# A convolution by blocked Fourier transforms: the second copy of the weights loaded in four transfers of 49 partial rows

## Chip, cores and metric

The kernel runs on one core of one Trainium2 chip. The metric is the device time of one execution in microseconds (us). Lower is better.

## What is computed

The input `x` has the shape 1 x 224 x 224 x 96, the weights `w` the shape 7 x 7 x 96 x 96, both bf16. The reference pads the weights to the image size, transforms both, multiplies per frequency with a sum over the input channels, and transforms back:

```python
wp = jnp.pad(w, ((0, H - K), (0, W - K), (0, 0), (0, 0)))
Xf = rfft2(x, axes=(1, 2)); Wf = rfft2(wp, axes=(0, 1))
Yf = jnp.einsum('bhwi,hwio->bhwo', Xf, Wf)
y = irfft2(Yf, s=(H, W), axes=(1, 2)).astype(bfloat16)
```

This is a circular 7 x 7 convolution with 96 input and 96 output channels.

## The kernel before

The kernel transforms only along the image rows' axis (height), in eight blocks of 28 output rows each, and does the width axis as short sums over the seven taps. The width of 224 is cut into seven strips of 32 columns (`t` = 0 to 6). For each strip TensorE first multiplies the rows of `x` with a table `Fm` (tiles `x0` and `xh`, which live in the last slots of `WF` and are shown as `WF` in the profile, and `xn`), and ScalarE or VectorE copy the result to `xf`. VectorE forms sums and differences of `xf` in the `J` tiles. In 17 rounds per strip (`b_round`, one for each frequency) TensorE multiplies `xf` and `J` with the transformed weights `WF`. The result `yf` goes to a scratch tensor in DRAM (`scr`), comes back with another arrangement (`tt`), is multiplied with the table `Gm`, and is stored to `out`.

The transformed weights are made at the start. The 49 taps of `w` are 49 rows of 96 x 96 elements, 18,432 bytes each. They are loaded twice into the tile `wq` (`wqx` in the code), which has 128 partitions:

- The first copy stands in partitions 30 to 78 (from `W1`). Twelve wide jobs (`wide_jobs`, line 397) read partitions 0 to 78 of it with a table of factors and fill the weights of the first frequencies.
- The second copy stands in partitions 79 to 127 (from `K1`). It is shifted by 48 columns, so that its row has 9,168 elements (`WC`, 18,336 bytes) instead of 9,216. The jobs of `prep_jobs` (line 415) read all 128 partitions and so both copies at once, eight output channels in four matmuls. They make the weights of the later frequencies.

Both copies are loaded by two helpers. `load_w` (line 192) moves `n` whole rows in one transfer. `load_last` (line 196) moves the last row, cut into 16 runs, in two transfers of half a run each. The kernel before calls each with 48 rows and the last row.

All these loads are issued by SyncE (SP) on its one queue, in the order of the code: first half of the rows of strip 0 (`x0`), the first copy, the halos, the other half of strip 0, the two halves of strip 1 (`xn`), and as the last the second copy. Each half of a strip is a transfer of 112 rows and one of 6 rows. After the second copy the queue holds the first stores of `yf`.

TensorE's order is written out in the code (the `_Ordered` wrapper keeps each engine's program order). Warm-up matmuls, the transforms of strip 0 and the wide jobs come first. Then the rounds start, and other jobs are placed between them by `pace` (line 786): a list of jobs is given a first and a last step, and the jobs are spread evenly over the steps between. The first of the `prep_jobs` comes at step 4, in the third round, with the transforms of strip 1 around it. Its matmul is TensorE's first reader of the second copy.

The profile puts nearly all instructions on line 101, the line of the wrapper, so groups are told apart by their tiles.

Of the kernel before, what the change touches and what calls it, by code (L numbers as in the profile page):

```python
# [66 lines left out]
def kernel(  # L67
# [7 lines left out]
    _, H, W, C = x.shape  # L75
# [5 lines left out]
    PW = KT * KT  # L81
    FR = 2 * NS
    EP = 128
    K1 = W1 + PW
    assert K1 + PW == EP and len(S5) == PGRP[0][1]
    C2 = C // 2
# [59 lines left out]
    def dma(out_ap, in_ap):  # L146
        return DE.dma_start(out=out_ap, in_=in_ap)
# [18 lines left out]
    wqx = wtmp.tile([128, C - 1 + 127 * C + 1], BF16, name="wq")  # L166
    WC = C * C - C2
# [19 lines left out]
    def load_x(t, jg):  # L187
        return load_rows(xbuf(t, jg), jg, t * 2 * TW, 2 * TW)

    wsrc = w.rearrange("kh kw i o -> (kh kw) (i o)")  # L190

    def load_w(p, k, n, h):
        m = (C * C, WC)[h]
        return dma(wqx[p:p + n, 0:m], bass.AP(wsrc.tensor, wsrc.offset + k * C * C + h * C2, [[C * C, n], [1, m]]))

    def load_last(p, h):
        n = (C * C, WC)[h]
        m = n // 16
        for a, b in ((0, m // 2), (m // 2, m)):
            dma(wqx[p:p + 1, 0:n].rearrange("p (c m) -> p c m", c=16)[:, :, a:b],  # L200
                bass.AP(wsrc.tensor, wsrc.offset + (PW - 1) * C * C + h * C2 + a, [[C * C, 1], [m, 16], [1, b - a]]))

    load_x(0, 0)
    load_last(K1 - 1, 0)
    load_w(W1, 0, PW - 1, 0)
    for jg in range(2):
        load_rows(xh_bufs[jg], jg, W - PAD, PAD)
    load_x(0, 1)
    for jg in range(2):
        load_x(1, jg)  # L210
    load_w(K1, 0, PW - 1, 1)
    load_last(EP - 1, 1)

    wu = cpool.tile([128, 128], BF16, name="wu")
    wur = wu[:].unsqueeze(1).to_broadcast([128, 4, 128])
# [717 lines left out]
    for i, (g, q) in enumerate(order):  # L933
# [3 lines left out]
        k = i + 8 - LF  # L937
# [37 lines left out]
```

## Time and profile before

| What | Value |
|---|---|
| median of 3 runs | 270.6 us (270.03 to 270.99) |
| profiled execution, its own time | 269.31 us |
| its span from first to last instruction | 267.5 us |
| granted TensorE clock, mean | 0.995 |
| PE (matmul) busy | 255.1 us, 95% |
| DVE busy | 216.2 us, 81% |
| ACT busy | 197.6 us, 74% |
| first copy, issue of its whole rows | 864.0 KB in one transfer |
| second copy, issue of its whole rows | 859.5 KB in one transfer |
| issue of the second copy's three transfers on SP | from 11.69 us, 3.29 us in all |

Times in the profile count from the start of the span. PE is TensorE's matmul, PEld its weight load, DVE VectorE, ACT ScalarE, POOL GpSimd, SP SyncE. In a timeline, the bracket behind a piece is the time that the engine stood idle before it, and what ended that; "issue" is a wait that the profile can't name. A table of windows gives for each stretch its length, the busy time and count of each engine, the granted clock, and at the end the mean busy share of the 16 DMA engines and the GB/s. A packet's bytes and its time are counted where it starts, so a share can pass 1 in a short window.

### The profile page before, as it was taken

The page shows a single profiled execution, that of the slowest core. Times are in us where ns is not written, and L with a number is a line of the kernel's source. Part 1 is how long each engine was busy: PE and PEld are TensorE (multiplying, and loading weights), DVE is VectorE, ACT ScalarE, POOL GpSimd, SP SyncE. Part 2 cuts the span into 40 slices and gives each one's busy share as a digit, 9 for nine tenths or more (in the row PEclk, how much of TensorE's full clock was granted, in tenths as well). Part 3 has the DMA queues.
Part 4 walks back from the last instruction along what each step waited for, and adds up shares of the span by engine and source line. Part 5 has one row for each costly group of instructions (what it writes and reads, how often), then busy time and mean ns, then how long its engine had stood idle before and what let it go on. Part 6 is the DMA issues. An engine that isn't in the chain of part 4 may idle for free. (4 is left out here: it accounts for less than half of the span.)

```text
span 267.5 us, 12139 instructions
## 1 busy us (share of the span) xinstructions
PE 255.1 (95%) x5128; PEld 235.7 (88%) x5128; DVE 216.2 (81%) x465; ACT 197.6 (74%) x485; POOL 97.7 (37%) x152
## 2 busy tenths in 40 slices
PE   8897999999999999999999999999999999999983
PEld 2787999999998999999999998989999889879861
DVE  7997699889899788778887888778888789978523
ACT  8796978497964578998988789886988864187123
POOL 7771324364558344222222322233123323422100
PEclk9999999999999999999999999999999999999998
DMA  8994102711111697987876486979678443887845
GB/s 197 230 251 76 48 2 67 245 45 48 47 48 49 192 258 159 294 238 223 272 195 188 117 235 221 253 216 341 235 152 242 169 128 125 204 250 182 259 107 191
DMA packets 46690, 46.78 MB, mean 175 GB/s; under 512 B 35292, under 2 KB 38056, under 8 KB 46540
## 3 DMA queue, kind: packets, MB, share of 16 engines
q1 hardware_dynamic: 44348, 43.95, 59.6%
q10 hardware_dynamic: 2288, 2.06, 2.6%
q8 instruction: 40, 0.66, 1.1%
q14 instruction: 14, 0.11, 0.2%
HBM read 24.66 MB, written 21.33 MB: 172 GB/s over the span
## 5 line engine op out<-in xcount | busy, mean ns | idle before, releaser
L101 PE MATMUL pb<-WF,J 96*128 96x96 bf16 x2821 | 162.9, 206 | 1.7 <-DVE J L101 1.3
L101 PEld LDWEIGHTS <-J 96*128 96x128 bf16 x2821 | 138.0, 98 | 12.3 <-issue 3.5
L101 POOL TENSOR_TENSOR yf<-v,u 128x384 bf16<-128x384 f32 x79 | 81.3, 1040 | 145.7 <-issue 84.6
L101 ACT CAST xf<-pb 96x408 bf16<-96x408 f32 (+3 forms) x145 | 67.3, 486 | 7.6 <-PE pb L101 3.8
L101 PE MATMUL pb<-WF,xf 96*128 96x96 bf16 x952 | 60.0, 206 | 0.9 <-ACT WF L101 0.9
L101 DVE TENSOR_TENSOR J<-xf 96x1824 bf16<-96x1824 bf16 (+1 forms) x84 | 56.9, 716 | 0.0
L101 PEld LDWEIGHTS <-xf 96*128 96x128 bf16 x952 | 47.2, 98 | 1.3 <-issue 1.2
L101 PE MATMUL pb<-Fm,xn 118*128 118x136 bf16 (+3 forms) x640 | 45.5, 199 | 0.2 <-DVE u L101 0.2
L101 PE MATMUL pb<-tt,Gm 102*84 102x384 bf16 (+1 forms) x132 | 32.9, 326 | 0.6 <-ACT J L101 0.3
L101 PEld LDWEIGHTS <-xn 118*128 118x128 bf16 x640 | 30.3, 97 | 0.3 <-issue 0.3
L101 ACT CAST WF<-pb 96x480 bf16<-96x480 f32 (+1 forms) x58 | 28.6, 558 | 2.3 <-PE pb L101 2.3
L101 ACT CAST J<-pb 84x384 bf16<-84x384 f32 (+1 forms) x65 | 28.1, 490 | 2.6 <-PE pb L101 2.6
L101 ACT CAST yo<-pb 84x384 bf16<-84x384 f32 (+1 forms) x63 | 27.1, 486 | 2.3 <-POOL yf L101 1.3
L101 DVE TENSOR_TENSOR J<-J 96x912 bf16<-96x912 bf16 (+2 forms) x42 | 24.2, 576 | 0.0
L101 PE MATMUL pb<-wq 128*128 128x120 bf16 (+1 forms) x288 | 21.8, 226 | 0.7 <-DMA wq<-in_w_dram 0.6
L101 PEld LDWEIGHTS <-wq 128*128 128x128 bf16 (+1 forms) x288 | 19.9, 148 | 1.7 <-DVE xf L101 1.1
L101 DVE TENSOR_TENSOR yf<-v,u 128x384 bf16<-128x384 f32 x26 | 15.1, 580 | 0.9
L101 PE MATMUL pb<-wu 128*112 128x384 bf16 (+1 forms) x59 | 14.5, 391 | 1.1 <-DVE ct L101 1.1
L101 PEld LDWEIGHTS <-wu 128*112 128x112 bf16 (+1 forms) x59 | 7.4, 127 | 5.6 <-issue 3.1
L101 PEld LDWEIGHTS <-Gm 102*84 102x84 bf16 (+1 forms) x132 | 11.1, 117 | 1.0 <-issue 0.4
L101 ACT COPY xf<-xf 96x816 bf16<-96x816 bf16 (+3 forms) x20 | 11.1, 613 | 0.0
L101 ACT CAST tt<-pb 112x384 bf16<-112x384 f32 x8 | 3.6, 480 | 9.3 <-PE pb L101 9.2
(387 smaller groups left out, 239.2 us busy)
## 6 DMA issues: line engine op xcount, KB each, us to landing
scr<-yf SPq DMA_DIRECT2D x30, 288.0 KB
xn<-in_x_dram SPq DMA_DIRECT2D x12, 672.0 KB
tt<-scr SPq DMA_DIRECT2D x24, 336.0 KB
out_dram<-yo SPq DMA_DIRECT2D x12, 252.0 KB
out_dram<-J SPq DMA_DIRECT2D x12, 252.0 KB
tt<-scr SPq DMA_DIRECT2D x6, 288.0 KB
WF<-in_x_dram SPq DMA_DIRECT2D x2, 672.0 KB
out_dram<-tt SPq DMA_DIRECT2D x8, 168.0 KB
```

Of the source, the lines that this page charges most:

```text
L101: r = fn(*a, **k)
```

## The change

The second copy is loaded by four transfers. Each moves all 49 rows (partitions 79 to 127) and a quarter of the columns, 2,292 elements or 4,584 bytes per row. The two transfers of the last row's pieces go away for this copy. `load_w` gets the column bounds as arguments. The first copy is loaded as before.

```diff
-    def load_w(p, k, n, h):
-        m = (C * C, WC)[h]
-        return dma(wqx[p:p + n, 0:m], bass.AP(wsrc.tensor, wsrc.offset + k * C * C + h * C2, [[C * C, n], [1, m]]))
+    def load_w(p, k, n, h, m0=0, m1=C * C):
+        return dma(wqx[p:p + n, m0:m1], bass.AP(wsrc.tensor, wsrc.offset + k * C * C + h * C2 + m0, [[C * C, n], [1, m1 - m0]]))
...
-    load_w(K1, 0, PW - 1, 1)
-    load_last(EP - 1, 1)
+    for i in range(4):
+        load_w(K1, 0, PW, 1, i * WC // 4, (i + 1) * WC // 4)
```

## Prediction

> **What bounds the kernel now.** I read the page first, then the windows by stage, the waits of PE, and the timeline around the first reader of the second copy. The page's first lines name the bound:
>
> ```profile
> span 267.5 us, 12139 instructions
> PE 255.1 (95%) x5128; PEld 235.7 (88%) x5128; DVE 216.2 (81%) x465; ACT 197.6 (74%) x485; POOL 97.7 (37%) x152
> ```
>
> From 27.3 to 233 us PE waits for named things this often and no more (the waits of PE in that window), and it is busy for 203.70 of the 205.80 us (windows by stage: length, PE, PEld, DVE, ACT, POOL, clock, DMA share, GB/s):
>
> ```profile
> PE pb L101 <- DVE J L101: 1.3, 3, 0.5
> PE pb L101 <- DVE u L101: 0.4, 2, 0.2
> 27.20:233.00 205.80, 203.70 (x4345) 194.32 (x4346) 174.11 (x362) 160.35 (x404) 75.91 (x76) 1.00 0.60 170
> ```
>
> So what PE gains or loses near 27 us reaches the end nearly one for one: the chain that ended last runs over PE until 239.10 us, then over the last stores and loads of the scratch. The place that the change touches is in the timeline:
>
> ```profile
> 23.67 0.41 PE L101 MATMUL pb<-Fm,WF 118*128 118x40 bf16 x10
> 25.30 0.50 PE L101 MATMUL pb<-Fm,WF 118*128 118x32 bf16 x14 [1.23 <-issue]
> 26.59 0.35 PEld L101 LDWEIGHTS <-J 96*128 96x128 bf16 x7
> 27.20 0.81 PEld L101 LDWEIGHTS <-wq 128*128 128x128 bf16 x12 [0.25 <-DMA wq<-in_w_dram]
> ```
>
> The reader is to see two things. The first reader of the second copy really waits for its load: PE is ready at 26.95, the last completion is at 27.14 in the trace's landing records, the load starts at 27.20. The copy is 0.25 us late today, so any lateness is paid by PE. And 1.9 us earlier PE stands 1.23 us on "issue".
>
> **On how many engines a transfer runs.** In the first 31 us the DMA view counts
>
> ```profile
> DMA packets 1102, 5.06 MB, mean 163 GB/s; under 512 B 228, under 2 KB 528, under 8 KB 1000
> ```
>
> No data packet there is under 512 B, so 228 are completion writes, one per engine used: six transfers of 112 rows and two of 48 with 16 each, six of 6 rows with 6, four of 16 pieces with 16, 96 + 32 + 36 + 64 = 228. For other row counts I take the page's 35,292 packets under 512 B: 32,384 are 384-byte pieces (scratch reloads: 24 x 112 x 8 + 6 x 68 x 12 + 12 x 34 x 4 + 2 x 72 x 16 + 32 x 16 + 2 x 96 x 8) and 200 are 56-byte pieces of GA and GB. That leaves 2,708, which is exactly what comes out if every transfer uses the largest divisor of its rows up to 16 (84 rows 14, 34 rows 2); one engine per row up to 16 would give 3,000. So **49 rows run on 7 engines**, and 48 ran on 16. [...]
>
> **The change part by part.**
> *Removed:* one transfer of 48 x 18,336 B (3 rows per engine) and two of 16 pieces. *Added:* 4 x 49 packets of 4,584 B, 28 per engine on seven engines: 898,464 B / 7 = 128.4 KB instead of 55 KB each. Order and number of instructions on PE, DVE, ACT and POOL stay; the first reader waits on four semaphores instead of three, which I cost at nothing (below 0.05 us).
>
> *SP:* three issues took 3.29 us from 11.69 with a wait in them; a fourth is 0.3 to 0.6 us (issue rows) and ends near 15.5. That is hidden, for the DMA engines come to the second copy only from 17.2 (first 18,336 B packet). Behind it SP has a store that it can't issue before 31.29. If that cover were gone, 0.6 us.
>
> *When the seven engines can start.* The packet records show nine engines with their first packet of the second copy from 17.24 to 17.86 and seven from 19.16 to 20.85. [...] From 18.0 each late engine has about 4.3 rows of 6 KB left; today they go at 12 to 16 GB/s beside nine engines that already write the second copy. [...]
>
> *Rate of one engine.* Nothing before shows seven engines on this data alone. Bounds from windows, GB/s / (16 x share):
>
> ```profile
> 4.20:9.60 5.40, 5.05 (x106) 3.40 (x104) 4.74 (x17) 4.86 (x7) 4.25 (x22) 1.00 0.98 211
> 9.60:17.20 7.60, 7.00 (x115) 6.26 (x114) 7.02 (x14) 5.76 (x13) 5.99 (x26) 1.00 1.04 263
> 20.90:26.00 5.10, 3.87 (x115) 3.79 (x113) 3.25 (x7) 3.03 (x10) 0.78 (x1) 1.00 0.34 55
> 22.70:26.00 3.30, 2.07 (x66) 1.99 (x64) 2.03 (x4) 2.03 (x7) 0.00 (x0) 1.00 0.25 50
> 144.50:146.00 1.50, 1.50 (x38) 1.50 (x36) 1.47 (x3) 1.31 (x5) 0.00 (x0) 1.00 0.28 103
> ```
>
> First copy 13.5; rows of `x` with all engines busy 15.8; second copy today 10.1, its last part, on the late engines, 12.5; a tail with some 4.5 engines busy 23.0. I take 23.0, since only seven of 16 engines will be busy: the last second-copy packet that ran nearly alone took 0.749 us (24.5 GB/s), so the data itself is not slow. [...]
>
> [...]
>
> *Sum.* From the last packet to completion takes 1.2 us today (25.93 to 27.14). 19.4 + 128.4 / 23.0 (5.6) + 1.2 = **26.2 us**, 0.9 us before today's landing. PE gains the 0.25 us wait. What is late next is "issue": PE's fetch queue (q8, 40 packets of 16 KB, 256 instructions each) had a packet from 22.28 that took 1.69 us, where undisturbed ones take 0.95; PE stood until 25.30. If that packet's engine is not among the seven, up to 0.74 us of the stall goes too. Bounds 0 and 0.74; I take 0.15, because VectorE is behind PE there (busy 28.87 of 32.80 us from 27.20 to 60.00) and would hand part of it back, and because a landing at 26.2 leaves nothing to spare. Total -0.25 - 0.15 = -0.4 us, so 268.9 for the profiled execution (269.31: span 267.5 and 1.8 around it). It lies 1.3 below the median; set on the median, **270.2 us**.
>
> **Rivals.**
> 1. *The seven engines become the bound (slower).* Lateness is nothing until the landing passes 27.14, that is below 128.4 / 6.54 = 19.6 GB/s. At 15.8 the landing is 28.7 (+1.6 us, 272.2); at 13.5, 30.1 (+3.0, 273.6); at 12.5, 30.9 (+3.7, 274.3); at 10.1, 33.3 (+6.2, 276.8). For it: these are the rows of this stage, the last-but-one with this very data and about seven engines. Against: the 0.749 us packet, and the nearly empty queues. [...]
> 2. *The fetch stall goes as well (faster).* -0.25 - 0.74 = -1.0, 269.6. For it: the fetch lengthened just when the second copy's large packets were under way. Against: the landing must then come by 26.2.
> 3. *The transfers use 16 engines after all.* Then the load is as today: 0 to -0.25, 270.5. Against: the count of 2,708.
>
> **How the numbers follow.** 0.3% is 0.8 us, about what a measurement of this kernel can tell from no change. Forecast (landing before about 28, part of the fetch stall) 0.40, rival 3 0.03, both within 0.3%. Rival 1 by more than 0.8 us (below 17.5 GB/s): 0.34. Rival 2, more than 0.8 us gained: 0.23. Range: down to 269.4, rival 2 and a little; up to 273.5, rival 1 at 13.5 GB/s, which leaves the slower rows outside with about 0.12 and 0.08 below. The likeliest case's own range is 269.8 to 271.4.
>
> **What would show it.** Right: 208 packets under 512 B in the first 31 us (228 - 48 + 28; 16 engines would give 244); the first weight load from `wq` with 128 partitions without a DMA wait before it; no DMA traffic but fetches after some 25.5 us. The fetch step: "issue" before the 25.30 matmul falls from 1.23 to about 0.5. Wrong: a wait on "DMA wq<-in_w_dram" of over 1 us in front of that load, with DMA traffic at 70 to 110 GB/s until 28 us or later.

## Result and the profile after

| | Before | After |
|---|---|---|
| first pair: median of 6 and 6 runs | 270.47 us (269.08 to 272.44) | 268.0 us (266.91 to 268.23) |
| ratio | | 0.9896, 95% interval 0.9854 to 0.9937 |
| profiled execution: time, span, granted clock | 269.31, 267.5, 0.995 | 267.92, 266.1, 0.999 |

The change made the kernel faster. The changed kernel was run in two more sets, beside new runs of the kernel before: 0.9954 [0.9921, 0.9987] and 0.9934 [0.9902, 0.9967]. The first ratio is the most favourable of the three. The granted clock differs a little between runs, on average 0.9953 in 90 runs of the kernel before and 0.9972 in 29 of the changed one; executions in the chip's slower state are left out of these averages, the ratios and the fits. A fit to the spans of 192 runs of this study, with one term for each kernel and one for the granted clock, gives the change -1.03 us (standard error 0.16) at equal clock, about -0.4%; the same fit to the device times gives -1.20 (0.17).

The clock term may take away part of the effect: in the two first profiles the granted clock is 1.00 until TensorE has done its last matmul (262.79 and 261.34 us) and falls to 0.50 only after it, at 264.88 and 265.34, so the mean also depends on how long the kernel goes on from there. Without the clock term the fits give -1.39 (0.22) on the spans and -1.56 (0.22) on the device times. The gain is thus some 1.0 to 1.6 us. Single differences of one microsecond between two profiles mean little here; stages have to be compared.

The page of the changed kernel, its first lines:

```profile
span 266.1 us, 12141 instructions
PE 254.9 (96%) x5128; PEld 235.7 (89%) x5128; DVE 216.2 (81%) x465; ACT 197.3 (74%) x485; POOL 98.3 (37%) x152
```

The DMA view of its first 31 us:

```profile
DMA packets 1198, 5.06 MB, mean 163 GB/s; under 512 B 208, under 2 KB 476, under 8 KB 1144
q1 hardware_dynamic: 1192, 4.97, 60.0%
```

The 208 small packets are the prediction's 228 - 48 + 28: by this count, one small packet per engine and transfer, each of the four transfers runs on seven engines. The packets of the data queue q1 took 60.0% of the time of 16 engines in the window; before it was 70.7%, for the same bytes.

The timeline at the place of the change (start, duration, engine, work, and in the bracket the idle time before it):

```profile
23.20 0.76 PE L101 MATMUL pb<-Fm,WF 118*128 118x40 bf16 x24
23.80 0.63 PE L101 MATMUL pb<-Fm,xn 118*128 118x64 bf16 x16
...
24.78 0.46 PE L101 MATMUL pb<-WF,J 96*128 96x96 bf16 x7
26.32 0.81 PEld L101 LDWEIGHTS <-wq 128*128 128x128 bf16 x12 [1.22 <-issue]
26.35 0.92 PE L101 MATMUL pb<-wq 128*128 128x120 bf16 x12 [1.11 <-DMA wq<-in_w_dram]
```

The stall of 1.23 us on "issue" ahead of the 25.30 matmul is gone: no piece from 23.20 to 24.78 has a bracket. PE now arrives at the first reader of the second copy 1.11 us early and stands there until the copy lands. The idle time has changed its place and its cause, and the reader starts at 26.35 instead of 27.23. The windows by stage (length, PE, PEld, DVE, ACT, POOL, clock, DMA share, GB/s) show the copy on seven engines in the second and third row. The kernel before moved 55 and 50 GB/s there, the changed one moves 113 and 87 with about the same busy share of the engines (0.32 and 0.26 against 0.34 and 0.25), so each busy engine moves 2.2 and 1.7 times as much (an estimate from these shares):

```profile
9.60:17.20 7.60, 7.13 (x121) 6.64 (x120) 7.42 (x15) 6.09 (x13) 5.99 (x26) 1.00 1.02 265
20.90:26.00 5.10, 4.34 (x127) 4.19 (x124) 3.26 (x7) 4.49 (x12) 0.42 (x1) 1.00 0.32 113
22.70:26.00 3.30, 2.54 (x76) 2.39 (x72) 2.50 (x5) 3.16 (x9) 0.00 (x0) 1.00 0.26 87
27.20:233.00 205.80, 203.72 (x4349) 194.16 (x4347) 174.68 (x363) 159.39 (x402) 75.91 (x76) 1.00 0.60 171
```

The waits of PE from 27.2 to 233 us are the same as before:

```profile
PE pb L101 <- DVE J L101: 1.3, 3, 0.5
PE pb L101 <- DVE u L101: 0.4, 2, 0.2
```

Because PE executes the same 5,128 matmuls in the same order in every kernel here, the start of the n-th matmul cuts all executions into the same stages. The table gives the stages of one profiled execution each, in us (matmul 120 lies in the work on the first copy, 400 just behind the first reader of the second, 5050 at 250 us):

| Kernel | start of 120 | 120 to 800 | 800 to 5050 | 5050 to last |
|---|---|---|---|---|
| before | 11.16 | 32.74 | 205.70 | 12.86 |
| before, second profile | 11.01 | 32.33 | 205.74 | 12.67 |
| changed | 10.73 | 32.31 | 205.71 | 12.26 |
| changed, second profile | 10.54 | 32.84 | 205.73 | 13.16 |
| changed, third profile | 11.19 | 31.26 | 205.73 | 13.04 |
| 49 whole rows, one transfer | 10.88 | 31.65 | 205.75 | 13.57 |
| changed, copy issued earlier | 10.77 | 31.34 | 205.72 | 12.74 |
| the same, second profile | 11.02 | 31.37 | 205.70 | 13.40 |

Two things follow. Between 800 and 5050 the rows shown agree within 0.05 us, so what PE wins near 27 us it keeps to 249 us. Of the other runs, only the one with 48 rows in quarters differs by more than a tenth: its profile has 206.58 us there, with a wait of 0.7 us for `tt` from the scratch that no other profile has. And the first and last stage vary by 0.7 and 1.3 us between executions of kernels that do the same there: of the 1.4 us between the two first spans, 0.43 is there before the change can act, 0.43 belongs to the stage of the change and 0.60 to the tail, where the wait for `xf` from the scratch was 0.3 instead of 0.9 us.

### The profile page after: what moved, and what is told of

It reads as the page before. It is cut to its first block, busy times and chain, and to the rows that moved or that the text cites. A ratio compares the mean times of both kernels' runs of the same rounds, so it can differ in the third digit from the quotient of the medians.

```text
span 266.1 us, 12141 instructions
## 1 busy us (share of the span) xinstructions
PE 254.9 (96%) x5128; PEld 235.7 (89%) x5128; DVE 216.2 (81%) x465; ACT 197.3 (74%) x485; POOL 98.3 (37%) x152
```

## Experiments

**The kernel before, unchanged.**

> The kernel before, unchanged, timed against itself and profiled again. It shows how the two places that changed (the stall on issue ahead of the 25.30 us matmul, 1.23 us, and the wait for the second copy, 0.25 us) vary from one execution to the next, and the spans of its timed runs. Theory E (engines): the seven late engines include the one that fetches PE's instructions, so a stall of 0.8 to 1.5 us plus a wait of 0 to 1.5 us is in every execution; the first reader of the second copy starts between 27 and 29 us. Theory N (mostly noise): the first reader moves by over 1 us between executions for reasons at the start of the kernel, and the ratio 0.9896 is half noise. Ratio expected 1.000 by both.

Measured: 270.15 us, ratio 1.002 [0.9977, 1.0063], so the comparison shows no difference where there is none. Its first reader starts at 26.45, ahead of the 27 to 29 us of theory E, since the copy landed in time in this execution. Its timeline has the stall again, with another size:

```profile
24.83 0.50 PE L101 MATMUL pb<-Fm,WF 118*128 118x32 bf16 x14 [0.91 <-issue]
```

**The changed kernel, unchanged.**

> The changed kernel, unchanged, timed again on the same chip as the others. Theory E: ratio 0.988 to 0.994, first reader near 26.3 us with no stall on issue before it. Theory N: ratio 0.995 to 0.998, first reader anywhere from 26 to 27.5 us.

Measured: 268.57 us, ratio 0.9954 [0.9921, 0.9987]. No "issue" stall; the wait for `wq` was 1.50 us and the reader started at 26.71. The place is as theory E expected it, but the ratio lies in the range of theory N: the first ratio was probably in part noise.

**One transfer of 49 whole rows**: the count of engines without the packet size.

```diff
-    for i in range(4):
-        load_w(K1, 0, PW, 1, i * WC // 4, (i + 1) * WC // 4)
+    load_w(K1, 0, PW, 1, 0, WC)
```

> One part of the change alone: 49 whole rows in one transfer, so seven engines, but packets of 18,336 B instead of quarters. Theory E (what counts is which engines carry the copy): as the changed kernel, ratio 0.988 to 0.994, no stall on issue near 24 us, landing near 26.3 us. Theory P (what counts is the size of the packets that the instruction fetch has to queue behind): the stall stays at 0.8 us or more and the ratio is 0.995 to 1.000.

Measured: 268.29 us, ratio 0.9932 [0.99, 0.9965]; at equal clock -1.17 us (0.25). The small packets are 208 - 28 + 7 = 187, one transfer on seven engines. No "issue" stall, and a wait of 0.40 us at the reader:

```profile
25.82 0.97 PE L101 MATMUL pb<-wq 128*128 128x120 bf16 x12 [0.40 <-DMA wq<-in_w_dram]
```

The column quarters are not needed for the gain. The row count is enough.

**48 rows in four column quarters**, the last row in pieces: the packet size without the count of engines.

```diff
-    load_w(K1, 0, PW - 1, 1)
+    for i in range(4):
+        load_w(K1, 0, PW - 1, 1, i * WC // 4, (i + 1) * WC // 4)
```

> The other part alone: 48 rows in four column quarters on 16 engines, with the last row in pieces as before; packets of 4,584 B. Theory E: the copy is as slow as before (nine engines early, seven late, landing 26.5 to 28 us), the stall on issue stays near 1.2 us, ratio 0.998 to 1.003. Theory P: the fetch packet near 22 us is as short as with the change (1.1 us instead of 1.7), the stall falls below 0.5 us, ratio 0.990 to 0.996.

Measured: 269.21 us, ratio 0.9969 [0.9937, 1.0001], between the two theories; at equal clock -0.26 us (0.24). The DMA view of the first 31 us counts 228 + 48 = 276 small packets, so the quarters ran on 16 engines each:

```profile
DMA packets 1314, 5.11 MB, mean 165 GB/s; under 512 B 276, under 2 KB 576, under 8 KB 1259
```

The stall remains, at about half its size:

```profile
24.18 0.50 PE L101 MATMUL pb<-Fm,WF 118*128 118x32 bf16 x14 [0.54 <-issue]
```

A packet of 4,584 B took 0.396 us on average here, 11.6 GB/s per engine, and 0.204 to 0.209 us in the changed kernel, 22 GB/s. So the smaller packets do not set the rate. Whether they bring a quarter to half of a microsecond (the fit to the device times has -0.49, with 0.24) or nothing can't be told from these runs.

**Eight whole rows per transfer**, last row in pieces. The engines of this run and of those with 42 and 7 rows (eight, 14 and seven) are an estimate, from the divisor that the counts of 208, 187 and 276 small packets bear out.

```diff
-    for i in range(4):
-        load_w(K1, 0, PW, 1, i * WC // 4, (i + 1) * WC // 4)
+    for i in range(6):
+        load_w(K1 + 8 * i, 8 * i, 8, 1)
+    load_last(EP - 1, 1)
```

> Second copy as six transfers of 8 whole rows (8 engines each, one more than 49 rows use) and the last row in pieces as before. [...]

Measured: 273.34 us, ratio 1.0107 [1.0059, 1.0155]. No "issue" stall, but a long wait for the copy:

```profile
29.82 1.38 PE L101 MATMUL pb<-wq 128*128 128x120 bf16 x12 [4.24 <-DMA wq<-in_w_dram]
```

The second packet of the fetch of PE's instructions started at matmul 232, at 17.46 us, when the first packet of the copy (17.37) had only just begun. The loss is the copy itself, 13.0 GB/s per engine (mean of its 18,336 B packets, 1.415 us), and what comes with the long wait: the granted clock is 0.50 from 27.71 to 34.53 us, and matmul 400 to 800 takes 18.12 instead of 16.47 us. In this version each of the six transfers writes eight neighbouring partitions, and SP needs 11.46 us for the eight issues; single issues of the copy took 0.31 to 0.51 us in the kernel before, so most of this is waiting (an estimate). The two runs with seven rows below take these apart.

**42 rows on 14 engines and 7 rows on 7.**

```diff
-    for i in range(4):
-        load_w(K1, 0, PW, 1, i * WC // 4, (i + 1) * WC // 4)
+    load_w(K1, 0, 42, 1)
+    load_w(K1 + 42, 42, 7, 1)
```

> Second copy as one transfer of 42 whole rows (14 engines) and one of 7 rows (7 engines). [...]

Measured: 269.59 us, ratio 0.998 [0.9944, 1.0016]. Its profiled execution ran at a granted clock of 0.981 and was late from its start (span 271.6), so its stall and its landing are not comparable: the second fetch packet started at matmul 217 and no "issue" stall followed, but PE came to its 349th matmul only 6.5 us after that packet had ended. Which engine does the fetch can't be read from it. The copy ran at 11.5 GB/s per engine. Of the gain, nothing is left that these runs could show.

**The changed kernel with the second copy issued ahead of the second half of strip 1.**

```diff
-    for jg in range(2):
-        load_x(1, jg)
+    load_x(1, 0)
     for i in range(4):
         load_w(K1, 0, PW, 1, i * WC // 4, (i + 1) * WC // 4)
+    load_x(1, 1)
```

> The changed kernel with the second half of strip 1 (112 + 6 rows) issued after the second copy instead of ahead of it. With the stall gone, the three runs on seven engines wait 0.4 to 1.5 us for the second copy, so its landing is the bound there. Theory E: it now lands some 2 us sooner, before 25.2 us, the wait goes, the first reader starts at 25.0 to 25.4 us, and the kernel gains 0.7 to 1.3 us more than the change: ratio 0.988 to 0.993. Rival (the half strip becomes the late one): its first reader at about 29 us waits instead, and the ratio stays at 0.993 to 0.997.

Measured: 267.66 us, ratio 0.9904 [0.9869, 0.9939]. Neither stall nor wait is left, as theory E expected; the reader starts at 25.22:

```profile
24.92 0.46 PE L101 MATMUL pb<-WF,J 96*128 96x96 bf16 x7
25.22 0.90 PE L101 MATMUL pb<-wq 128*128 128x120 bf16 x12
```

**The same exchange in the kernel before.**

```diff
-    for jg in range(2):
-        load_x(1, jg)
+    load_x(1, 0)
     load_w(K1, 0, PW - 1, 1)
     load_last(EP - 1, 1)
+    load_x(1, 1)
```

> The kernel before with the same exchange of order: copy on 16 engines, 48 whole rows and pieces, ahead of the second half of strip 1. Theory E: the wait for the copy (0 to 0.25 us) goes, but the fetch engine still has as much queued on it, so the stall on issue stays at 0.5 to 1.2 us: ratio 0.998 to 1.001. Rival (the lateness of the copy alone is what the change cured): as the changed kernel or better, ratio 0.990 to 0.995.

Measured: 271.49 us, ratio 1.003 [0.9998, 1.0062]; at equal clock +0.93 us (0.23). The last data packet of the copy ends at 23.04 instead of 25.83 us, and yet PE loses more:

```profile
27.12 0.50 PE L101 MATMUL pb<-Fm,WF 118*128 118x32 bf16 x14 [2.82 <-issue]
29.51 1.40 PE L101 MATMUL pb<-wq 128*128 128x120 bf16 x12
```

This is the run that decides between the two explanations of the gain. An earlier copy alone gains nothing, and by the fit it costs: on 16 engines PE had done 348 matmuls and stood before the second packet of its fetch even started, at 24.60 us. What the change cured was not the copy's lateness but the lateness of this packet. The profiled execution is the slowest of the 12, so its stall is larger than most; and behind it the granted clock is 0.50 from 27.86 to 31.27 us, which adds to the loss (matmul 400 to 800 takes 16.99 us).

**Seven adjacent rows per transfer**, seven transfers.

```diff
-    for i in range(4):
-        load_w(K1, 0, PW, 1, i * WC // 4, (i + 1) * WC // 4)
+    for i in range(7):
+        load_w(K1 + 7 * i, 7 * i, 7, 1, 0, WC)
```

> Seven transfers of 7 whole adjacent rows take the place of the change's four; the pieces stay away. [...] Theory A (what made the run with 8-row transfers slow was that engines write neighbouring partitions): the rate falls from the change's 22 GB/s per engine to the 10 to 13 of the copy before, the landing comes at 29 to 31 us, and the time is 1.5 to 4 us above that of the changed kernel, and clearly above the run with stride-7 rows beside it. Theory B (it was only that SyncE issues the later transfers late, each behind a transfer eight places earlier): rate per engine about 22 GB/s whenever a transfer is under way, landing the same as in the stride-7 run within 0.3 us, 26.5 to 29 us.

Measured: 271.03 us, ratio 1.0044 [1.0008, 1.0081]; at equal clock +1.07 us (0.28). The profiled execution is the fastest of the ten, with 269.04 us, so it doesn't show where the others lose their time. No stall, the reader at 27.50:

```profile
25.76 0.46 PE L101 MATMUL pb<-WF,J 96*128 96x96 bf16 x7
27.50 0.92 PE L101 MATMUL pb<-wq 128*128 128x120 bf16 x12 [1.27 <-DMA wq<-in_w_dram]
```

**The same with every seventh row per transfer.**

```diff
-        load_w(K1 + 7 * i, 7 * i, 7, 1, 0, WC)
+        dma(wqx[K1 + i:K1 + PW:7, 0:WC], bass.AP(wsrc.tensor, wsrc.offset + i * C * C + C2, [[7 * C * C, 7], [1, WC]]))
```

> [...] Both theories: rate per engine about 22 GB/s. Theory A: landing 1.5 to 4 us before that of the adjacent run. Theory B: the same landing within 0.3 us; if both land after 27.5 us with gaps between the packets, the cause is the late issue.

Measured: 290.59 us, ratio 1.0753 [1.069, 1.0815]. This time says nothing about the question: ScalarE stood for 23.75 us until the copy had landed before it filled its own part of `wq`, the table `Fm` came from VectorE behind that, and PE waited for `Fm`:

```profile
PE pb L101 <- DVE Fm L101: 23.4, 1, 23.4
```

Only its packets can be used, with the caution that PE stood still beside them. They took 0.797 us on average, 23.0 GB/s per engine, against 0.876 us or 20.9 GB/s for adjacent rows and 0.792 us or 23.1 GB/s in the one transfer of 49 rows. The last data packet ended at 25.44, with adjacent rows at 26.77. Neither theory is borne out: adjacency costs about 10% of the rate, not half of it, and yet the landing is 1.3 us apart. Of these, 7 packets x 0.08 us = 0.6 us are the rate; the first packet of the run with adjacent rows was 0.8 us later (18.04 against 17.22), an execution that was late already at matmul 120 (11.69 us, against 10.88 in the run of 49 whole rows). So neighbouring rows explain little of the slowness on eight engines.

**The exchange and the change side by side.**

> The change with the second half of strip 1 issued after the second copy, again, beside the changed kernel on one chip. The copy then lands before TensorE is ready for it, so the 1.1 to 1.5 us wait in front of its first reader goes. Theory A (TensorE passes on what it gains there nearly whole): 0.7 to 1.3 us below the changed kernel. Theory B (the end is set elsewhere as well): within 0.4 us of it.

> The changed kernel unchanged, as the partner of the run with the exchange. Expected 0.8 to 1.5 us below the kernel before, a ratio of 0.9945 to 0.997.

Measured: 267.66 us with the exchange, ratio 0.9916 [0.988, 0.9952]; 267.97 us without, 0.9934 [0.9902, 0.9967]. The difference of 0.3 us is inside what these runs resolve; the 0.7 to 1.3 us of theory A did not come, and the changed kernel was a little faster than expected for it. One reason is that in this execution of the changed kernel the copy landed in time, with its last data packet at 24.81 instead of 25.62 and 25.92 us:

```profile
25.27 0.46 PE L101 MATMUL pb<-WF,J 96*128 96x96 bf16 x7
25.73 0.91 PE L101 MATMUL pb<-wq 128*128 128x120 bf16 x12
```

Over all runs the fit gives the exchange -1.76 us (0.21) against the kernel before, 0.73 us more than the change alone. This was the fastest version, but its lead over the changed kernel rests on the fit, not on a direct comparison.

## Why the prediction was wrong

The forecast was 270.2 us, no difference; measured were 268.0, and a gain of some 1.0 to 1.6 us in the long run. The second rival, "the fetch stall goes as well", was what happened, at a chance of 0.23, but not by its sum: more of the stall went than it had allowed, and the wait for the copy did not go.

- *49 rows on seven engines*: right, by the count of 208. The largest divisor of the rows up to 16, which the prediction found in the count of 2,708, agrees with more counts (187, 276, and 208, 209 and 208 in the three profiles of the change). The prediction saw in the smaller number of engines mainly a risk (rival 1, at 0.34), and here it was the gain.
- *Start of the seven at 19.4*: no run shows this term as such, since the packet records name no engine. They show in the first profile of the change the first packet of the copy at 17.54 us, no more than two under way at a time until 18.6, and seven first at 19.21, so 19.4 was near enough.
- *Rate 23.0 GB/s*: measured 21.9 to 22.5 per engine in three profiles. Rival 1, with its lower rates, did not occur. (At 13.5 GB/s its own sum gives 273.6 us, not the 273.5 of the range.)
- *Landing at 26.2*: the reader started at 26.35, 26.71 and 25.73 in three profiles. Two errors cancel in the first: the last data ended at 25.62, not at 25.0 (19.4 + 5.6), and from there to the reader it took 0.73, not 1.2 us.
- *The wait of 0.25 us goes*: wrong. It was replaced by a wait of 1.11 us for the same copy, because PE comes earlier by the whole stall. The prediction had named a wait of over 1 us there as a sign that its forecast was wrong, by reason of a slow copy; it appeared with a fast copy.
- *The fetch stall, "I take 0.15"*: this is the step that failed. The price was read from the length of the fetch packet alone, 1.69 against 0.95 us, which bounded it at 0.74, and of that only 0.15 was taken. The whole stall of 1.23 us went. The packet was 0.62 us shorter, 1.07 instead of 1.69, but it also started 1.75 us earlier, and for that the prediction had no term. The second fetch packet, by the packet records:

| Kernel | starts at us | took us | PE is then at matmul | 349th matmul starts at | stall on "issue" |
|---|---|---|---|---|---|
| before | 22.28 | 1.69 | 303 | 25.30 | 1.23 |
| before, again | 21.88 | 1.54 | 296 | 24.83 | 0.91 |
| 48 rows in quarters | 21.29 | 1.51 | 284 | 24.18 | 0.54 |
| before, exchange | 24.60 | 1.15 | 348 | 27.12 | 2.82 |
| changed, three profiles | 20.53, 20.78, 17.77 | 1.07, 1.08, 1.25 | 266, 276, 234 | 23.45, 23.43, 23.95 | none |
| 49 whole rows | 17.75 | 1.21 | 238 | 23.64 | none |
| 8 rows, eight engines | 17.46 | 1.27 | 232 | 23.79 | none |
| changed, exchange, two profiles | 20.70, 20.57 | 1.08, 1.37 | 267, 260 | 23.59, 23.76 | none |
| 7 adjacent rows | 18.24 | 1.22 | 234 | 24.43 | none |
| 42 and 7 rows, late from its start | 22.01 | 1.29 | 217 | 29.84 | none |

The stall follows the end of the packet. All four stalls stand in front of the same matmul, the 349th, and it starts 1.33 to 1.41 us after the packet's end; in every other profile PE comes there 1.56 us or more after it. So the length counts as much as the start, but the starts differ more, and the largest stall has one of the shorter packets. Every profile with the copy's whole transfers on 16 engines stalls, and none with seven or eight does. The run with every seventh row, in which PE stood still for 23.4 us ahead of all this, is left out.

Why the packet comes sooner is only partly shown. The records name no engine, but the packets of the copy that are under way at a time can be counted. In both profiles of the kernel before there were never fewer than seven while the fetch packet moved, which speaks against its having run on one of the seven late engines, as theory E had it (an inference from the counts). It started only as the other nine came to their end: the mean count fell from about 14 just before it to 8 during it. With the change the obvious reading, that the seven leave the fetching engine free, is not borne out: in the first two profiles of the changed kernel and the first with the exchange, 6.1 copy packets on average were under way while the fetch packet moved, against 6.8 to 7.1 just before it, as if it took the place of one of the seven. In the second profile with the exchange it did not (7.2 against 7.1). So by these counts the prediction's condition, an engine that is not among the seven, was not needed. What is shown is that with seven engines the packet ended early enough (18.96 to 21.94 us), and with 16 it didn't (22.80 to 25.75); what sets its start stays open.

The two wrong terms nearly cancel in the first pair of profiles: -1.23 for the stall and +0.86 for the wait (1.11 instead of 0.25) make -0.37, where the forecast had -0.4. That is luck. In the third profile of the change the copy came in time, and the stage from matmul 120 to 800 took 31.26 us, against 32.31 and 32.84 with a wait and 32.74 and 32.33 in the kernel before.

- *"VectorE is behind PE there and would hand part of it back"*: nearly wrong. The changed kernel's lead of 0.87 us over the kernel before at matmul 400 is 0.86 at 800 and 0.85 at 5050. The most that was handed back in any profile where PE came earlier is in the run with the exchange, 16.70 instead of 16.47 us from matmul 400 to 800, so 0.23 us, and a second profile of the kernel before has 16.69 as well. VectorE's busy time was an average; where PE needs its results they were there.
- *"A landing at 26.2 leaves nothing to spare"*: right. It holds the gain of the change down. PE stood 1.11 and 1.50 us in two of three profiles.
- *The rest of the miss is variation.* Forecast and measurement lie 2.2 us apart. The forecast held -0.4 and the fits have -1.0 to -1.6, so 0.6 to 1.2 us is mis-sized effect; the other 1.0 to 1.6 us is how this set of six runs fell against the median of three, 270.6 us, that the forecast was set on. The kernel before itself came out between 269.63 and 270.54 us in the later sets.

What stays open. The profiles of the stage (120 to 800) give the change on average -0.4 us (32.14 in three against 32.54 in two), the timed runs -1.0 to -1.6; with a spread of 1.6 us between three profiles this is no contradiction, but it isn't a proof of the size either. The seven adjacent rows have no stall and are slower all the same, which their one profile doesn't explain. And the rate isn't explained. The kernel before moved only 65 to 81 GB/s from 23.0 to 24.0 us with seven engines still on the copy, 9 to 11 per engine; the transfers of eight rows moved 84 GB/s on eight engines at 20 us; the seven engines of the change moved 143 to 166 in its first profile, from 20 to 24 us. The transfers of eight rows themselves moved 110 to 117 GB/s from 23.5 to 25.5 us, and the run with seven adjacent rows never moved less than 121 GB/s while all seven engines were on the copy.

## What to carry to other kernels

Here a load of 898 KB on 16 DMA engines went with a late packet of the instruction fetch: it ended at 22.80 to 25.75 us, and TensorE, the busiest engine, stood 0.54 to 2.82 us. Where a trace shows "issue" ahead of a matmul and a late 16 KB packet in the fetch queue, a load on fewer engines is worth a try (here by 49 rows in a transfer instead of 48): on seven engines the copy landed as early (24.81 to 25.92 us), and the fetch packet ended at 18.96 to 21.94 with no stall, while transfers of eight rows made the kernel slower (273.34 us, ratio 1.0107). Price such a stall by when the fetch packet ends and when the engine comes to the instruction at which it stood, here the 349th matmul, not by how long the packet takes: the largest stall, 2.82 us, had a packet of 1.15 us. And when a stall ahead of a wait goes, look at once whether the wait takes its place, as the 1.11 us for the copy did here: the next step, issuing the copy earlier, gained 0.73 us by the fit on top of the change and cost 0.93 us without it.

## What the runs showed of the hardware that was not expected

- Seven engines delivered this copy as fast as sixteen: 898 KB had its last data packet at 24.81 to 25.92 us in the changed kernel, and the whole rows of the kernel before had theirs at 25.05 and 25.83 us.
- Four times PE stood without a named cause in front of the same matmul, the 349th, which then started 1.33 to 1.41 us after the end of the second packet of its instruction fetch. With 16 engines on the copy issued early, that packet started at 24.60 us, only when PE had already stopped, and PE stood for 2.82 us.
- In three profiles with the copy on seven engines the number of copy packets under way fell from about seven to 6.1 while the fetch packet moved, and PE had no stall.
- The same data to the same partitions ran at 10 to 13 GB/s per engine on 8, 14 or 16 engines and at 21 to 23 on seven (8 and 14 by the divisor); on seven engines beside rows of `x`, in the two profiles of the exchange, it was 18.5 and 14.5.
- Where PE stood for 2.82 and 4.24 us, the granted clock fell to 0.50 for 3.4 and 6.8 us; with stands of 1.11 to 1.50 us it stayed at 1.00.
